# Finishing a float64 conversion on VectorE, and float32 operands used directly in two batches' attention

## The chip, the cores and the metric

The kernel runs on one core of a Trainium2 chip. The metric is the device time of one launch in microseconds, as the median of several runs. The core's engines have short names in the profile: PE is TensorE (PEld its weight loads), DVE is VectorE, ACT is ScalarE, POOL is GpSimd and SP is SyncE, which here only issues transfers. Each engine works through its own list of instructions in order, and waits for the others by semaphores.

## The reference

Attention goes through 32 packs per head, and two feed-forwards follow it. The weights (`w_in`, `w_out`, `w1` to `w3` and the second `w_out`) are float64 arrays; q, k, v and p are float32.

```python
p_packed = sm_attn(p, k, v)            # 8 batches, 8 heads, 576 tokens, 64 wide, 32 packs
out = sm_attn(q, p_packed, p_packed)
x = out.transpose(0, 2, 1, 3).reshape(4608, 512)
h = x @ w_in                           # 512 x 2048
g = h * (1.0 / (1.0 + np.exp(-1.702 * h)))
x = g @ w_out                          # 2048 x 512
h = np.maximum(np.maximum(x @ w1, x @ w2), x @ w3)   # 512 x 768 each
return (h @ w_out2).astype(np.float32)
```

## The kernel before

A float32 product is made of three passes over exact halves: an operand is split into a high half (a ScalarE cast to float32r) and a low half (what is left, by a subtraction), and `mm3` (lines 91 to 94) issues low times high, high times low, and high times high. `split` (112 to 114) does the subtraction on GpSimd, `evac` (116 to 118) does it on VectorE for a product that leaves PSUM.

The attention of four heads of a batch is a `Group`. Its steps are: load p and k (`load_pk`), put p into a block-diagonal tile `pbd` and split k (`split_pk`), load v, the scores of the packs `s1` with their softmax `sm1`, split v, transpose the weights into `et` (`t1`, `t1r`), the packed values `pv`, load and split q, transpose the packed values into `pt` (`pt`), the scores of the tokens `s2`, their softmax (`sm2`, `sm3`), and a transpose into `at` (`tr2`), which is split too. There are 16 groups; those of batches 0 and 1 (four) come first.

The weights arrive as the raw bits of float64, 1024 numbers per partition at a time. `convert` makes the two halves of such a block: four VectorE instructions over 1024 elements (lines 135, 138, 141, 143), two ScalarE instructions (136, 146), and two more over 1024 elements that finish the low half: an integer addition (147) on GpSimd and a subtraction (148) on GpSimd, or on VectorE in the first three blocks. Four blocks are needed for each quarter of the first feed-forward's hidden features (`wi0_n`, `wi1_n`, and two `wo`): 16 in all, and 12 blocks of the second feed-forward follow later (`tmp_w`).

The first feed-forward runs over 256 units, each of 288 tokens and 128 hidden features. `h_unit` makes the products `h` (6 matmuls, from `at` and from `pw`, the packed values times the first weights), a tanh on ScalarE (443) and a multiplication on VectorE (444). `g_unit` splits the result into two halves, with the cast on ScalarE (449) and the subtraction on VectorE (450). `out_unit` adds 12 matmuls to the accumulators `acc`. Batches 0 and 1 take turns in the first 128 units, so that conversions can keep up. The second feed-forward has 54 units of `h2_unit` and `out2_unit`.

All steps are written into a plan with a time each and issued in the order of these times; the tables `D_`, `W_`, `K_`, `L_` and others set them, and they are the same before and after. The tile framework then orders the instructions of each engine by its own estimate of their costs. Buffers come from pools: `w` (16 tiles, for raw weights, scratch and converted halves), `u` (18 tiles), and `ur` (6 tiles, for raw k, v and q).

Of the kernel before, what the change touches and what calls it, by code (L numbers as in the profile page):

```python
# [8 lines left out]
F32 = mybir.dt.float32  # L9
# [30 lines left out]
def tile_packed_attention_moe(  # L40
# [31 lines left out]

    # [128, 2, 2, 512]: the halves of two float32 operands, or scratch
    def w_tile(name, dt=F32R):
# [13 lines left out]

    # float32 products as three passes of exact 12-bit halves: lo*hi + hi*lo + hi*hi
    def mm3(o, a, b, start, stop):  # L90
# [4 lines left out]

# [1 line left out]
    ident = const.tile([P, P], F32, name="ident")  # L97
# [12 lines left out]

# [1 line left out]
    def split(raw, hi, lo):  # L112
# [6 lines left out]

    # A float64 is sign, 11 bits of exponent and 52 of fraction. Its high half is the sign, the  # L120
    # exponent moved to float32's bias (0 below its range) and 11 bits of fraction; with the next
    # bits, rounded to 12, added to its last place it is the float32, and the low half is the rest.
    def load_raw(name, srcs):
# [5 lines left out]
    def convert(name, raw, pool):  # L129
        h = raw.rearrange("p x a (b w) -> p (x a b) w", w=2)[:, :, 1]  # L130
        m = raw.bitcast(U16).rearrange("p x a (b w) -> p (x a b) w", w=4)[:, :, 1]
        tmp = w_tile(f"tmp_{name}", I32)
        t1, t2 = (tmp[:, x].rearrange("p a b -> p (a b)") for x in range(2))
        w = w_tile(name)
        nc.vector.tensor_scalar(out=t1, in0=h, scalar1=0x7FFFFE00, scalar2=None, op0=ALU.bitwise_and)
        nc.scalar.activation(t1, t1, AF.Relu, scale=8.0, bias=rebias)
        yield
        nc.vector.tensor_scalar(
            out=t2, in0=h, scalar1=0x1FF, scalar2=3, op0=ALU.bitwise_and, op1=ALU.logical_shift_left
        )  # L140
        nc.vector.scalar_tensor_tensor(out=t2, in0=m, scalar=2.0 ** -13, in1=t2, op0=ALU.mult, op1=ALU.add)
        yield
        nc.vector.scalar_tensor_tensor(
            out=t1, in0=h, scalar=-2 ** 31, in1=t1, op0=ALU.bitwise_and, op1=ALU.bitwise_or
        )
        nc.scalar.copy(w[:, :, 0], f(tmp[:, 0]))
        nc.gpsimd.tensor_tensor(out=t2, in0=t2, in1=t1, op=ALU.add)
        (nc.vector if pool & 1 else nc.gpsimd).tensor_tensor(
            out=w[:, :, 1], in0=f(tmp[:, 1]), in1=f(tmp[:, 0]), op=ALU.subtract
        )  # L150
        yield w

# [1 line left out]
    at = {}  # L154
# [3 lines left out]
    class Group:  # L158
# [8 lines left out]

        def split_pk(self):
            t = u_tile(f"pbd_{self.n}", F32R)
            nc.gpsimd.memset(f(t), 0.0)  # L170
# [14 lines left out]
        def load_t(self, src, name):  # L185
            raws = []
            for c in range(2):
                raws.append(ur_tile(f"raw_{name}_{self.n}_{c}"))
                nc.sync.dma_start(raws[-1], src[self.b, 2 * self.g + c])
            return raws  # L190
# [9 lines left out]
        def load_v(self):  # L200
            self.vraw = []
            for c in range(3):
                raw = ur_tile(f"raw_v_{self.n}_{c}")
                if c < 2:
                    nc.sync.dma_start(raw[:, :TB], v[self.b, self.g, :, c])
                else:
                    nc.sync.dma_start(raw[D:, :2 * P], vr[self.b, self.g])
                self.vraw.append(raw)

        def split_v(self):  # L210
            self.v = []
            for c in range(3):
# [11 lines left out]

        def split_q(self):
            self.q = self.split_t(self.qraw, "q")

        # scores of the packs, [4 heads x 32 packs, 288 keys]
        def s1(self, hf):
            o = pa_tile(f"s1_{self.n}_{hf}")  # L230
            hs = slice(hf * HALF, hf * HALF + HALF)
            for c in range(2):
                mm3(
                    o[:, :HALF], [t[:, c * P:c * P + P] for t in self.pbd],
# [24 lines left out]

        # weights of the packs with keys on partitions  # L260
        def t1(self):
            self.et = [ap_.tile([P, 5 * P], F32R, tag=f"et{x}", name=f"et{x}_{self.n}") for x in range(2)]
            o = pa_tile(f"t1_{self.n}")
            for c in range(4):
                nc.tensor.transpose(o[:, c * P:c * P + P], self.e1[:, c * P:c * P + P], ident)
            evac(o, self.et[0][:, :TB], self.et[1][:, :TB])

        def t1r(self):
            o = pa_tile(f"t1r_{self.n}")
            nc.tensor.transpose(o[:, :P], self.e1[:, S - P:S], ident)  # L270
            evac(o[D:, :P], self.et[0][D:, TB:], self.et[1][D:, TB:])

        # packed values, block-diagonal over the four heads
        def pv(self):
            o = pa_tile(f"pv_{self.n}")
            for c in range(5):
                r = slice(D if c == 4 else 0, P)
                vs = slice(c % 2 * 2 * P, c % 2 * 2 * P + 2 * P)
                mm3(
                    o[:, :2 * P], [t[r, c * P:c * P + P] for t in self.et],  # L280
# [7 lines left out]
        def pt(self):  # L288
# [6 lines left out]
            if self.b < 2:  # L295
                ptt[self.b, self.g] = self.ptt
                return
            # beside the packs of the other batch of the pair
            key = self.b // 2, self.g
# [8 lines left out]

        # scores of the tokens, [4 heads x 32 packs, 288 tokens], then tokens on partitions
        def s2(self, hf):  # L310
            o = pa_tile(f"s2_{self.n}_{hf}")
            hs = slice(hf * HALF, hf * HALF + HALF)
            for c in range(2):
                mm3(
                    o[:, :HALF], [t[:, c * P:c * P + P] for t in self.ptt],
# [26 lines left out]

        # weights of the tokens with packs on partitions
        def tr2(self):
# [5 lines left out]

        # (delay in us, step) of the whole group
        def steps(self):
# [4 lines left out]

# [1 line left out]
    wi = {}  # L359
# [20 lines left out]

    # the same for one batch
    def pw1_unit(b, g, n):
# [14 lines left out]

# [1 line left out]
    wo = {}  # L399
    gt, acc = {}, {}  # L400

    # units of the first feed-forward: (batch, half of its tokens, chunk of hidden features). Batches
    # 0 and 1 take turns by ranges of the chunks, so that the weights' conversions keep up.
    PAT = {
# [78 lines left out]

# [1 line left out]
    w3, wo2 = {}, {}  # L485
# [56 lines left out]

# [1 line left out]
    plan = []  # L544
# [36 lines left out]
    def main():  # L581
        HU = 2.2
        T0 = 39
        # startup
        attention(0.0, 0, 0, 1.07)
# [53 lines left out]

        # first feed-forward  # L640
        for pr in range(1, B // 2):
# [14 lines left out]

        # second feed-forward
        def w2_store(fc, x):
# [83 lines left out]
```

## Time and profile before

| | before |
|---|---|
| median of 3 runs | 1472.63 us (1471.9 to 1473.1) |
| span of the profiled execution | 1471.5 us |
| PE busy | 1391.3 us (95%), 8178 matmuls |
| PEld busy | 1257.4 us (85%) |
| DVE busy | 814.9 us (55%), 1355 instructions |
| ACT busy | 548.1 us (37%) |
| POOL busy | 421.2 us (29%), 351 instructions |

The span runs from the first to the last instruction of the profiled execution. Its own time is not recorded apart from that; the shown runs stand 0.4 to 1.6 us above the span. The busy shares are averages over a start, in which attention and conversions run, and a long remainder, in which hardly anything but matmuls goes on; they must be read stage by stage.

### The profile page before, as it was taken

How to read it: one execution, taken by the hardware profiler on the slowest of the kernel's cores; microseconds unless marked ns; L12 is line 12 of the kernel's file. 1: busy time of each engine (PE TensorE's matmuls, PEld its weight loads, DVE VectorE, ACT ScalarE, POOL GpSimd, SP SyncE). 2: the span in 40 equal slices, each digit the busy share in tenths (PEclk: the TensorE clock that was granted, in tenths of full speed). 3: DMA queues.
4: the chain of work that ended last, by engine and by line, in shares of the span. 5: the costliest groups of instructions: out<-in, count | busy, mean ns of one | idle time of the engine just before them, and what ended most of it. 6: DMA issues, size and time to landing. Idle time of an engine off the chain costs nothing.

```text
span 1471.5 us, 20929 instructions
## 1 busy us (share of the span) xinstructions
PE 1391.3 (95%) x8178; PEld 1257.4 (85%) x8178; DVE 814.9 (55%) x1355; ACT 548.1 (37%) x1134; POOL 421.2 (29%) x351
## 2 busy tenths in 40 slices
PE   3698788999999999999999999999999999999998
PEld 2587788999999999999999888888888888888887
DVE  6989998787675767666447997212122222222222
ACT  4454455555554555555444543112111111112011
POOL 7755675533431233520002466101011010101000
PEclk9799899999999999999999999999999999999999
DMA  7453323354323233332112232101010110100000
GB/s 251 166 187 138 143 90 90 121 176 121 119 80 97 93 96 98 92 102 88 60 55 94 86 137 92 59 4 57 0 58 15 43 29 29 43 0 30 1 29 29
DMA packets 53475, 121.42 MB, mean 83 GB/s; under 512 B 7296, under 2 KB 16512, under 8 KB 53376
## 3 DMA queue, kind: packets, MB, share of 16 engines
q1 hardware_dynamic: 44288, 86.52, 17.7%
q0 software_dynamic: 9088, 33.56, 6.9%
q8 instruction: 64, 1.05, 0.3%
q14 instruction: 35, 0.29, 0.1%
HBM read 92.80 MB, written 27.26 MB: 82 GB/s over the span
## 4 chain that ended last, share of the span: by engine, by line
PE 77%; DVE 16%; issue 3%; ACT 2%; POOL 2%; DMA 1%; SPq 0%; POOLq 0%; ACTq 0%; DVEq 0%
PE hb L94 10%; PE hb L93 10%; PE hb L92 10%; PE acc L92 7%; PE acc L93 7%; PE acc L94 7%; PE h L92 3%; PE accb L94 3%; PE accb L92 3%; PE accb L93 3%; PE h L94 3%; PE h L93 3%; DVE g L450 3%; DVE t L444 1%; DVE pw L118 1%
## 5 line engine op out<-in xcount | busy, mean ns | idle before, releaser
L92 PE MATMUL acc<-g,wo 128*128 128x288 f32 x1024 | 307.6, 301 | 3.8 <-ACT g L449 1.4
L93 PE MATMUL acc<-g,wo 128*128 128x288 f32 x1024 | 303.9, 297 | 6.6 <-DVE g L450 6.5
L94 PE MATMUL acc<-g,wo 128*128 128x288 f32 x1024 | 302.8, 296 | 0.0
L518 DVE TENSOR_TENSOR m<-hb,m 128x512 f32<-128x512 f32 x108 | 74.7, 691 | 393.0 <-PE hb L94 392.7
L94 PE MATMUL hb<-x,w 128*128 128x512 f32 x648 | 252.1, 389 | 0.0
L93 PE MATMUL hb<-x,w 128*128 128x512 f32 x648 | 252.1, 389 | 0.0
L92 PE MATMUL hb<-x,w 128*128 128x512 f32 x648 | 252.1, 389 | 0.0
L93 PEld LDWEIGHTS acc<-g,wo 128*128 128x128 f32 x1024 | 195.1, 191 | 11.9 <-DVE g L450 9.3
L450 DVE TENSOR_TENSOR g<-t,g 128x288 fp32r<-128x288 f32 x254 | 169.4, 668 | 61.9 <-ACT g L449 58.3
L92 PEld LDWEIGHTS acc<-g,wo 128*128 128x128 f32 x1024 | 194.8, 190 | 9.7 <-ACT g L449 2.5
L94 PEld LDWEIGHTS acc<-g,wo 128*128 128x128 f32 x1024 | 194.7, 190 | 0.3
L92 PE MATMUL h<-at,pw 128*128 128x288 f32 x512 | 155.6, 304 | 11.7 <-DVE t L444 11.0
L449 ACT CAST g<-t 128x288 fp32r<-128x288 f32 x256 | 110.6, 432 | 140.8 <-DVE t L444 139.8
L114 POOL TENSOR_TENSOR x<-x2raw,x 128x512 fp32r<-128x512 f32 x36 | 50.2, 1426 | 380.2 <-ACT x L113 380.2
L444 DVE SCALAR_TENSOR_TENSOR t<-t,h 128x288 f32<-128x288 f32 x256 | 114.9, 449 | 77.8 <-ACT t L443 76.0
L443 ACT ACTIVATE t<-h 128x288 f32<-128x288 f32 x256 | 104.7, 410 | 136.6 <-PE h L94 135.0
L93 PE MATMUL h<-at,pw 128*128 128x288 f32 x512 | 152.5, 298 | 1.4 <-POOL at L114 1.4
L94 PE MATMUL h<-at,pw 128*128 128x288 f32 x512 | 152.4, 298 | 0.0
L92 PEld LDWEIGHTS hb<-x,w 128*128 128x128 f32 x648 | 121.7, 188 | 25.2
L94 PEld LDWEIGHTS hb<-x,w 128*128 128x128 f32 x648 | 121.6, 188 | 25.3
L93 PEld LDWEIGHTS hb<-x,w 128*128 128x128 f32 x648 | 121.6, 188 | 25.2
L92 PEld LDWEIGHTS h<-at,pw 128*128 128x128 f32 x512 | 97.6, 191 | 14.8 <-DVE t L444 12.5
(133 smaller groups left out, 2324.2 us busy)
## 6 DMA issues: line engine op xcount, KB each, us to landing
wi<-wsc POOLq DMA_DIRECT2D x48, 512.0 KB, 3.6
raw_k<-in_k SPq DMA_DIRECT2D x32, 288.0 KB, 3.0
raw_q<-in_q SPq DMA_DIRECT2D x32, 288.0 KB, 2.8
x2d<-x SPq DMA_DIRECT2D x16, 576.0 KB, 3.4
x2raw<-x2d SPq DMA_DIRECT2D x36, 256.0 KB, 2.7
raw_w<-in_w SPq DMA_DIRECT2D x18, 512.0 KB, 4.3
out<-o SPq DMA_DIRECT2D x36, 256.0 KB, 2.1
raw_wi<-in_w_in SPq DMA_DIRECT2D x16, 512.0 KB, 6.8
```

Of the source, the lines that this page charges most:

```text
L92: nc.tensor.matmul(o, al, bh, start=start, stop=False)
L93: nc.tensor.matmul(o, ah, bl, start=False, stop=False)
L94: nc.tensor.matmul(o, ah, bh, start=False, stop=stop)
L114: nc.gpsimd.tensor_tensor(out=lo, in0=raw, in1=f(hi), op=ALU.subtract)
L118: nc.vector.tensor_tensor(out=lo, in0=o, in1=f(hi), op=ALU.subtract)
L443: nc.scalar.activation(t, o, AF.Tanh, scale=0.5 * 1.702)
L444: nc.vector.scalar_tensor_tensor(out=t, in0=t, scalar=1.0, in1=o, op0=ALU.add, op1=ALU.mult)
L449: nc.scalar.copy(g[:, 0], gt[n])
L450: (nc.gpsimd if n < 2 else nc.vector).tensor_tensor(out=g[:, 1], in0=gt[n], in1=f(g[:, 0]), op=ALU.subtract)
L518: nc.vector.tensor_tensor(out=t, in0=o, in1=t, op=ALU.max)
```

## The change

Two things change. First, `convert`: the nine low bits of the float64's high word and the next 16 bits of its fraction become one float32 number of 25 bits (line 139 now multiplies the 16 bits by 2^-16 and adds the nine bits). A VectorE instruction masks sign and exponent out of the high half and writes them over the raw bits (145), and another multiplies the 25 bits by this power of two and by 2^-20 to give the low half (146). The two instructions that stood on GpSimd (147 and 148 of before, in three blocks one of them on VectorE) are gone.

Second, in batches 0 and 1 the attention's products take float32 operands as they are, in one matmul where there were three. k, v and q of these four groups are no longer split. `pbd` and `et` hold one float32 copy, and the transposed packed values get a float32 copy (`ptf`, in the buffer of `pbd`) beside their halves, which `pw1_unit` still needs. The raw v and q of these groups move from the pool `ur` to the pool `u`.

```diff
@@ convert
-        nc.vector.tensor_scalar(
-            out=t2, in0=h, scalar1=0x1FF, scalar2=3, op0=ALU.bitwise_and, op1=ALU.logical_shift_left
-        )
-        nc.vector.scalar_tensor_tensor(out=t2, in0=m, scalar=2.0 ** -13, in1=t2, op0=ALU.mult, op1=ALU.add)
+        nc.vector.tensor_scalar(out=t2, in0=h, scalar1=0x1FF, scalar2=None, op0=ALU.bitwise_and)
+        nc.vector.scalar_tensor_tensor(out=f(t2), in0=m, scalar=2.0 ** -16, in1=t2, op0=ALU.mult, op1=ALU.add)
...
         nc.scalar.copy(w[:, :, 0], f(tmp[:, 0]))
-        nc.gpsimd.tensor_tensor(out=t2, in0=t2, in1=t1, op=ALU.add)
-        (nc.vector if pool & 1 else nc.gpsimd).tensor_tensor(
-            out=w[:, :, 1], in0=f(tmp[:, 1]), in1=f(tmp[:, 0]), op=ALU.subtract
+        nc.vector.tensor_scalar(out=h, in0=t1, scalar1=-2 ** 23, scalar2=None, op0=ALU.bitwise_and)
+        nc.vector.scalar_tensor_tensor(
+            out=w[:, :, 1], in0=f(tmp[:, 1]), scalar=2.0 ** -20,
+            in1=f(raw).rearrange("p x a (b w) -> p x (a b) w", w=2)[:, :, :, 1], op0=ALU.mult, op1=ALU.mult
         )
@@ split_pk
+            if self.b < 2:
+                t = u_tile(f"pbd_{self.n}")
+                nc.gpsimd.memset(t[:, :2 * P], 0.0)
+                for x in range(2):
...
+                    nc.vector.tensor_copy(to, self.praw[r])
+                self.pbd = t
+                return
@@ load_t, load_v
-                raws.append(ur_tile(f"raw_{name}_{self.n}_{c}"))
+                raws.append((u_tile if self.b < 2 and name == "q" else ur_tile)(f"raw_{name}_{self.n}_{c}"))
...
-                raw = ur_tile(f"raw_v_{self.n}_{c}")
+                raw = (u_tile if self.b < 2 else ur_tile)(f"raw_v_{self.n}_{c}")
@@ split_v, split_q
+            if self.b < 2:
+                return
@@ s1 (pv and s2 alike, with et and vraw, ptf and qraw)
+                if self.b < 2:
+                    nc.tensor.matmul(
+                        o[:, :HALF], self.pbd[:, c * P:c * P + P], self.kraw[c][:, hs], start=c == 0, stop=c == 1
+                    )
+                    continue
@@ t1 (t1r alike)
+            if self.b < 2:
+                nc.scalar.copy(self.et[:, :TB], o)
+                return
@@ pt
+                self.ptf = self.pbd[:, :2 * P]
+                nc.scalar.copy(self.ptf, o[:, :2 * P])
```

On GpSimd, the first rows after the constants are these before. `k`, `v` and `q` are the low halves of group (batch, group of heads), and `tmp_` is the scratch of a conversion:

```order
L170 MEMSET pbd_0_107 128x576
L114 TENSOR_TENSOR k_0_0_0_114<-raw_k_0_0_103,k_0_0_0_113 128x576
L114 TENSOR_TENSOR k_0_0_1_118<-raw_k_0_1_105,k_0_0_1_117 128x576
L170 MEMSET pbd_1_153 128x576
L114 TENSOR_TENSOR k_0_1_0_160<-raw_k_1_0_149,k_0_1_0_159 128x576
L114 TENSOR_TENSOR k_0_1_1_164<-raw_k_1_1_151,k_0_1_1_163 128x576
L147 TENSOR_TENSOR tmp_wi_0_179<-tmp_wi_0_179 128x1024
L114 TENSOR_TENSOR v_0_0_0_206<-raw_v_0_0_167,v_0_0_0_205 128x512
L114 TENSOR_TENSOR v_0_0_1_210<-raw_v_0_1_169,v_0_0_1_209 128x512
L607 DMA wsc<-wi_0_180 128x2x1024
```

The same place of the change, which is also all that GpSimd has up to the second group's `at`:

```order
L170 MEMSET pbd_0_107 128x256
L170 MEMSET pbd_1_135 128x256
L645 DMA wsc<-wi_0_152 128x2x1024
L170 MEMSET pbd_0_257 128x256
L645 DMA wsc<-wi_0_283 128x2x1024
L114 TENSOR_TENSOR at_0_0_314<-at_0_311,at_0_0_313 128x576
L114 TENSOR_TENSOR at_0_1_403<-at_1_400,at_0_1_402 128x576
```

The splits and the conversion's addition have left this engine; memsets, stores and the split of `at` stay.

On VectorE, the end of the first conversion and the start of the second stand so before, between the second group's `pbd` and the first group's `et`:

```order
L141 SCALAR_TENSOR_TENSOR tmp_wi_0_179<-raw_wi_0_121,tmp_wi_0_179 128x1024
L180 CAST pbd_1_153<-praw_1_147 64x2x32
L255 TENSOR_SCALAR st_0_0_131<-st_0_0_131 128x1
L181 TENSOR_TENSOR pbd_1_153<-praw_1_147,pbd_1_153 64x2x32
L258 RECIPROCAL st_0_0_131<-st_0_0_131 128x1
L180 CAST pbd_1_153<-praw_1_147 64x2x32
L143 SCALAR_TENSOR_TENSOR tmp_wi_0_179<-raw_wi_0_121,tmp_wi_0_179 128x1024
L181 TENSOR_TENSOR pbd_1_153<-praw_1_147,pbd_1_153 64x2x32
L118 TENSOR_TENSOR et_0_0_190<-t_0_0_191,et_0_0_189 128x512
L118 TENSOR_TENSOR et_0_0_190<-t1r_0_198,et_0_0_189 64x128
L135 TENSOR_SCALAR tmp_wo_243<-raw_wo_173 128x1024
L148 TENSOR_TENSOR wi_0_180<-tmp_wi_0_179 128x2x512
```

In the change the same place reads:

```order
L139 SCALAR_TENSOR_TENSOR tmp_wi_0_151<-raw_wi_0_111,tmp_wi_0_151 128x1024
L263 TENSOR_SCALAR st_0_0_117<-st_0_0_117 128x1
L141 SCALAR_TENSOR_TENSOR tmp_wi_0_151<-raw_wi_0_111,tmp_wi_0_151 128x1024
L174 COPY pbd_1_135<-praw_1_129 64x2x32
L272 TENSOR_SCALAR st_0_0_117<-st_0_0_117 128x1
L174 COPY pbd_1_135<-praw_1_129 64x2x32
L145 TENSOR_SCALAR raw_wi_0_111<-tmp_wi_0_151 128x1024
L275 RECIPROCAL st_0_0_117<-st_0_0_117 128x1
L146 SCALAR_TENSOR_TENSOR wi_0_152<-tmp_wi_0_151,raw_wi_0_111 128x2x512
L135 TENSOR_SCALAR tmp_wo_193<-raw_wo_145 128x1024
```

The two instructions at 145 and 146 are new and finish the block at once; the subtractions for `pbd` (181) and `et` (118) are gone.

## Rows read from the trace of the kernel before

**Rows 1.** By stretch: busy PE, PEld, DVE, ACT, POOL; clock, DMA share, GB/s.

```profile
0.00:79.30 79.30, 39.17 (x165) 32.56 (x166) 63.27 (x82) 35.14 (x64) 57.89 (x48) 0.85 0.56 194
79.30:232.40 153.10, 128.82 (x811) 120.80 (x811) 146.38 (x200) 74.77 (x145) 95.39 (x54) 0.91 0.38 138
232.40:300.00 67.60, 65.67 (x462) 61.69 (x460) 51.88 (x113) 39.53 (x92) 34.74 (x39) 1.00 0.39 120
...
780.00:912.00 132.00, 126.66 (x824) 117.17 (x823) 115.72 (x160) 61.44 (x115) 66.17 (x28) 1.00 0.29 102
```

**Rows 2.** What PE waited for, 80 to 260 us: total us, times, longest.

```profile
PE h L92 <- DVE t L444: 10.5, 5, 4.4
PE acc L93 <- DVE g L450: 5.0, 5, 2.4
```

**Rows 3.** What DVE waited for, 0 to 80 us.

```profile
DVE pbd L180 <- POOL pbd L170: 5.0, 2, 2.9
```

**Rows 4.** Timeline of DVE around 132 us: start us, us, instruction.

```profile
132.07 2.53 DVE L135 TENSOR_SCALAR tmp_wo<-raw_wo 128x1024 int32<-128x1024 int32 x1
134.53 2.60 DVE L450 TENSOR_TENSOR g<-t,g 128x288 fp32r<-128x288 f32 x1
```

**Rows 5.** Timeline of POOL in the same place.

```profile
131.50 2.56 POOL L147 TENSOR_TENSOR tmp_wo<-tmp_wo 128x1024 int32<-128x1024 int32 x1 [9.90 <-DVE tmp_wo L141]
134.13 2.68 POOL L148 TENSOR_TENSOR wo<-tmp_wo 128x1024 fp32r<-128x1024 f32 x1
```

**Rows 6.** Single lines of DVE: count, duration in ns (least/median/most).

```profile
L450 DVE TENSOR_TENSOR g<-t,g x254: 416/459/2647, 88.4 to 878.0; 128x288 fp32r<-128x288 f32 x127
...
L138 DVE TENSOR_SCALAR tmp_wi<-raw_wi x8: 644/682/1747, 11.4 to 184.3; 128x1024 int32<-128x1024 int32 x8
...
L141 DVE SCALAR_TENSOR_TENSOR tmp_wi<-raw_wi,tmp_wi x8: 1210/1220/2424, 12.1 to 185.2; 128x1024 int32<-128x1024 uint16 x8
```

**Rows 7.** Instructions on `tmp_wi` by stretch: DVE, ACT and POOL us (count).

```profile
0.00:79.30 79.30, 13.97 (x10) 4.40 (x4) 4.77 (x2) 0.85 0.56 194
79.30:232.40 153.10, 31.69 (x24) 13.22 (x12) 30.79 (x12) 0.91 0.38 138
```

**Rows 8.** The same for `tmp_wo`.

```profile
0.00:79.30 79.30, 15.06 (x9) 4.39 (x4) 7.54 (x3) 0.85 0.56 194
79.30:232.40 153.10, 34.28 (x24) 13.18 (x12) 30.04 (x12) 0.91 0.38 138
```

**Rows 9.** The same for `tmp_w`, the second feed-forward's blocks.

```profile
780.00:912.00 132.00, 59.54 (x48) 26.45 (x24) 60.05 (x24) 1.00 0.29 102
```

**Rows 10.** DVE's groups by form, 0 to 79.3 us: count, busy us, mean ns.

```profile
L180 DVE CAST pbd<-praw 64x64 fp32r<-64x64 f32 x8 | 7.9, 984 | 5.6 <-POOL pbd L170 5.0 <-DMA praw<-in_p 0.4
L181 DVE TENSOR_TENSOR pbd<-praw,pbd 64x64 fp32r<-64x64 f32 x8 | 4.6, 569 | 0.2
...
L339 DVE TENSOR_TENSOR a<-a,st 128x576 f32<-128x576 f32 x2 | 3.4, 1724 | 0.1
```

**Rows 11.** Instructions on `et`, 0 to 79.3 us: PE, PEld, DVE, ACT.

```profile
0.00:79.30 79.30, 10.18 (x45) 9.23 (x45) 2.93 (x6) 2.54 (x6) 0.85 0.56 194
```

**Rows 12.** DVE's groups by form, 79.3 to 232.4 us.

```profile
L450 DVE TENSOR_TENSOR g<-t,g 128x288 fp32r<-128x288 f32 x34 | 34.7, 1027 | 1.3 <-ACT g L449 1.2
...
L327 DVE TENSOR_TENSOR a<-a,st 128x576 f32<-128x576 f32 x3 | 4.8, 1593 | 0.0
...
L339 DVE TENSOR_TENSOR a<-a,st 128x576 f32<-128x576 f32 x2 | 1.5, 746 | 0.0
...
L180 DVE CAST pbd<-praw 64x64 fp32r<-64x64 f32 x4 | 0.8, 189 | 2.2 <-POOL pbd L170 2.1
```

**Rows 13.** Timeline of PE near the start: two passes of a score, and four transposes.

```profile
8.50 0.44 PE L94 MATMUL s<-k,pbd 128*128 128x288 f32 x1
8.74 0.44 PE L92 MATMUL s<-k,pbd 128*128 128x288 f32 x1
...
12.88 1.17 PE L265 MATMUL t<-ident,e 128*128 128x128 f32 x4 [3.22 <-ACT e L251]
```

More of the change, by code (lines that the diff above doesn't have):

```diff
@@ L168, in split_pk @@
         def split_pk(self):
+            if self.b < 2:
+                t = u_tile(f"pbd_{self.n}")
+                nc.gpsimd.memset(t[:, :2 * P], 0.0)
+                for x in range(2):
+                    r = slice(D * x, D * x + D)
+                    to = t[r, :384].rearrange("p (a b) -> p a b", b=192)[:, :, NP * x:NP * x + NP]
+                    nc.vector.tensor_copy(to, self.praw[r])
+                self.pbd = t
+                return
             t = u_tile(f"pbd_{self.n}", F32R)
@@ L261, in t1 @@
         def t1(self):
-            self.et = [ap_.tile([P, 5 * P], F32R, tag=f"et{x}", name=f"et{x}_{self.n}") for x in range(2)]
+            if self.b < 2:
+                self.et = ap_.tile([P, 5 * P], F32, tag="et0", name=f"et_{self.n}")
+            else:
+                self.et = [ap_.tile([P, 5 * P], F32R, tag=f"et{x}", name=f"et{x}_{self.n}") for x in range(2)]
             o = pa_tile(f"t1_{self.n}")
@@ L265, in t1 @@
                 nc.tensor.transpose(o[:, c * P:c * P + P], self.e1[:, c * P:c * P + P], ident)
+            if self.b < 2:
+                nc.scalar.copy(self.et[:, :TB], o)
+                return
             evac(o, self.et[0][:, :TB], self.et[1][:, :TB])
@@ L270, in t1r @@
             nc.tensor.transpose(o[:, :P], self.e1[:, S - P:S], ident)
+            if self.b < 2:
+                nc.scalar.copy(self.et[D:, TB:], o[D:, :P])
+                return
             evac(o[D:, :P], self.et[0][D:, TB:], self.et[1][D:, TB:])
@@ L278, in pv @@
                 vs = slice(c % 2 * 2 * P, c % 2 * 2 * P + 2 * P)
+                if self.b < 2:
+                    nc.tensor.matmul(
+                        o[:, :2 * P], self.et[r, c * P:c * P + P], self.vraw[c // 2][r, vs], start=c == 0, stop=c == 4
+                    )
+                    continue
                 mm3(
@@ L313, in s2 @@
             for c in range(2):
+                if self.b < 2:
+                    nc.tensor.matmul(
+                        o[:, :HALF], self.ptf[:, c * P:c * P + P], self.qraw[c][:, hs], start=c == 0, stop=c == 1
+                    )
+                    continue
                 mm3(
```

## The prediction

> **What bounds the kernel now.** I read the busy time by stretch first, then the waits of the engine that idles, then single instructions. The stretches are cut where the work changes: at 79.3 us, where the first feed-forward product reaches DVE, and at 232.4 us, just after the last of the first 16 conversions. Call them A (0 to 79.3) and B (79.3 to 232.4). In A, PE is busy 39.2 of 79.3 us and DVE 63.3; in B, PE 128.8 of 153.1 us and DVE 146.4; from 232.4 on, PE is busy 65.7 of 67.6 us [rows 1]. So up to 232 us DVE has the most to do, and later PE does. The waits agree: in B, PE's longest are on DVE's product for h (10.5 us) and on its split of g (5.0 us) [rows 2]. What PE gains before 232 us is kept, for afterwards it is full whatever came before.
>
> Why DVE is so busy is seen in single instructions. The subtraction at line 450 takes 0.459 us in the middle and 2.647 at worst, with the same shape [rows 6]. At 132.07 us a mask (line 135) takes 2.53 us and the subtraction behind it 2.60 us [rows 4]; meanwhile POOL runs its two conversion steps, from 131.50 to 134.06 and from 134.13 to 136.81 [rows 5]. The mask ends at 134.60 and the subtraction at 137.13, each 0.3 to 0.5 us after a POOL instruction ended: about what such an instruction takes alone, or less. DVE stood there, counted as busy, until POOL was done. So part of DVE's 146.4 us is not work but POOL's time, and the change takes most of POOL's work away.
>
> **The change, part by part.** One profiled execution gives the durations. Its span is 1471.5 us, and the median of the runs is 1472.6, so I add 1.1 us at the end for what lies around the span.
>
> *Conversions.* A block had four DVE instructions and two on POOL. It now has six on DVE. Free of POOL, a mask over 1024 numbers takes 0.68 us (line 138's middle value) and a two-input instruction 1.22 us (line 141's) [rows 6]. The new mask (line 145) is shown nowhere: it writes every second word where lines 135 and 138 read every second word. Its ends are 0.68 us, as those, and 1.22 us, as the slowest instruction over 1024 numbers when undisturbed. I take 0.68, because it has line 135's layout turned round. The new multiplication (146) has a two-input instruction's row, 1.22. A block is then 3 x 0.68 + 3 x 1.22 = 5.7 us, at most 6.2.
> In A there are four blocks, which took DVE 14.0 + 15.1 = 29.0 us [rows 7, 8], the three subtractions at 148 within it; now 22.8: 6.2 saved. In B there are twelve, which took 31.7 + 34.3 = 66.0 us [rows 7, 8]; now 68.5: 2.5 lost, or 8.9 with the slow mask. Two more DVE instructions per block thus cost nearly nothing, if POOL leaves the others alone: of the 66.0 us, 66.0 - 12 x (2 x 0.68 + 2 x 1.22) = 20.4 was stretch.
>
> *Attention of batches 0 and 1.* In A, the copies and subtractions for `pbd` took 7.9 + 4.6 us [rows 10]. Eight copies at 0.19 us, as in B [rows 12], make 1.5: 11.0 saved. The `et` subtractions, 2.9 us for three groups [rows 11], go, and about 1.0 in B for the fourth. Line 339 falls from 3.4 us [rows 10] to two at 0.75 [rows 12]: 1.9 saved.
> On POOL, all splits of k, v and q of four groups go, so that memsets no longer stand behind them; DVE waited 5.0 us for such a memset in A [rows 3]. I count half of it, 2.5 us, since DVE then comes sooner to something else that is not there yet. ACT loses casts and gains one copy per group; with 35.1 of 79.3 us busy [rows 1] it hides that; uncovered, a copy would be worth less than one of the casts that go.
>
> *Other DVE work in B.* 34 subtractions at line 450 fall from 34.7 us [rows 12] to 34 x 0.459 = 15.6: 19.1 saved. Line 327 falls from 4.8 us to three at 0.75: 2.6 saved [rows 12]. The stretch in B is 19.1 + 20.4 + 2.6 = 42.1 us. It does not all go: of POOL's 95.4 us [rows 1] the conversions are 60.8 [rows 7, 8], and of the other 34.6, those for group (1, 1) go, while the splits of batches 2 and 3 stay. I keep a quarter of the stretch, 10.5 us (36%, 15.3 us, if all 34.6 stayed; nothing if they meet no DVE instruction).
>
> *Products.* 156 matmuls (39 for each of four groups) become 52. No row shows a float32 product of this size. A pass follows its neighbour by 0.24 us at the start [rows 13]; the nearest rows with float32 operands are the transposes, four in 1.17 us, at most 0.29 us for 128 columns [rows 13]. The ends are one pass, 0.24 us, and four passes, 0.96. Scaled by columns the transposes give 0.66 for 288, between them, and 0.66 for one is a little less than 0.72 for three passes. So I take no gain and no loss on PE, which has 40 idle us in A and 24 in B [rows 1]. The longer case is a rival below.
> The Trainium skill (FP8 and Floating Point Precision, TensorE Precision Notes) says that a true float32 product takes four passes through the array. No row shows it; by it, 52 products are 208 passes in place of 156, an estimate of 12 us more for PE at the early pace, and about 1444 us if half of that lies on the path.
>
> *Late conversions.* Twelve blocks fall between 780 and 912 us. They took DVE 59.5 us [rows 9] and will take 68.5, 9.0 more. DVE idles 132.0 - 115.7 = 16.3 us there [rows 1], and POOL's 60.1 us [rows 9] no longer stretch its neighbours. I count nothing; without that relief it would still fit, and with no idle time it would cost the 9.0.
>
> *Queues and buffers.* SP's loads of v and q no longer wait for POOL to release their `ur` tiles, and a raw weight tile is held until line 146 instead of 143, but POOL's steps, which held its scratch, are gone. I count both at nothing: earlier data only helps where DVE is not the last.
>
> **Sum.** A: 6.2 + 11.0 + 2.9 + 1.9 + 2.5 = 24.5 us. B: -2.5 + 1.0 + 19.1 + 2.6 - 10.5 = 9.7 us. Together 34.2: the span becomes 1437.3 us, and the time 1438.4 us, of which I say 1438. With the bounds (slow mask: 6.4 in B and 2.2 in A less; stretch kept 0 to 15.3; the memset wait 0 to 5.0) this case reaches from 1425 to 1454.
>
> **Rivals.**
> *PE or the loads set the start.* If a float32 product is four passes, a group's score, values and score take 8 x 0.96 + 5 x 0.85 = 12 us at the early pace instead of 39 x 0.23 = 9; three groups lie in A, one behind the other, and each step waits for a softmax. With 3 us each and as much again from DVE waiting for them, A gives about 9 less and B the same: 1447. Against it stands PE's idle half of A. Chance 20%.
> *PE takes over in B.* If the kept stretch is small and DVE's waits in A shrink too, PE becomes the bound in B. PE had 128.8 us there, in which a matmul is often slow or waits at a granted clock of 0.91; at the later pace (462 matmuls in 65.7 us [rows 1], 0.142 each) 811 take 115, which would save 38 in B; with waits between the engines I put it at 26, together 50: 1422. Chance 16%.
> *The stretch is not POOL's.* Then each of DVE's six instructions costs what one did on average. In A that is 29.0 / 19 = 1.53 us, 36.7 for 24, 7.7 more, which the 4.6 and 2.9 us of the subtractions that go make up for. In B, 66.0 / 48 = 1.37 us, so 24 new ones add 33, less 1.0. Late, 59.5 / 48 = 1.24 us, so 24 add 30 against 16.3 idle: 13. Together 45 slower, 1518 us. Between my 34 saved at a quarter kept and this, the sign changes when a little over half of the stretch stays. Rows 4 and 5 speak against it. Chance 6%.
> *The change does little*: the new steps run, but data or buffers hold the same places, within 0.2%: 2%.
>
> **How the numbers follow.** The main case has 56%. The predicted time is 1438 us. From 1414 to 1456 us lie the main case, the first rival and most of the second; what is left out is the deeper part of the second and the last two, and error in the sizes. 0.2% (3 us) is about what can be told from no change here. Faster 0.92, same 0.02, slower 0.06.
>
> **What would show it.** In the profile after, POOL has far less to do in the first 230 us, line 450's subtractions there take close to 0.46 us, the masks 0.68, line 145 too, and line 146 about 1.2. The first t comes about 25 us earlier, near 55 us, and the end of the sixteenth conversion some 34 us earlier, near 198. The prediction is wrong if DVE's instructions stay long with POOL quiet, if line 145 or 146 takes twice its row, or if PE waits for its own products in A.

## The result, and the profile after

| | before | after |
|---|---|---|
| median of 4 runs, us | 1472.27 (1470.53 to 1473.10) | 1436.82 (1434.98 to 1437.92) |
| profiled span, us | 1471.5 | 1433.0 |

The ratio is 0.976, 95% interval 0.9746 to 0.9773: 35.5 us faster, and 1 us below the 1438 forecast. The profiled execution took 1434.98 us, the fastest of its four, so its span is 38.5 shorter where the medians differ by 35.5: some 3 us between the two traces is the spread of the runs and not the change.

The first t reaches DVE at 59.1 us (79.3 before), and the last of the first 16 conversions is over at 203.9 (232.4 before). So A is now 0 to 59.1 and B 59.1 to 203.9. Busy time by stretch of the kernel after, in the columns of [rows 1], with the late conversions last:

```profile
0.00:59.10 59.10, 39.26 (x125) 25.53 (x125) 38.72 (x71) 22.79 (x44) 7.07 (x20) 1.00 0.76 273
59.10:203.90 144.80, 127.92 (x832) 118.39 (x832) 135.49 (x235) 79.39 (x157) 30.57 (x28) 0.96 0.41 145
...
741.00:872.00 131.00, 126.66 (x845) 120.23 (x844) 114.36 (x188) 62.88 (x118) 6.13 (x4) 0.99 0.30 103
```

In A, DVE's busy time fell by 63.3 - 38.7 = 24.6 us, but its idle time rose from 16.0 to 20.4, which leaves 20.2. In B it fell from 146.4 to 135.5. POOL fell from 57.9 to 7.1 in A and from 95.4 to 30.6 in B. What DVE waits for in A, beside [rows 3]:

```profile
DVE st L259 <- PE s L246: 5.5, 3, 3.8
DVE pbd L174 <- POOL pbd L170: 4.8, 2, 2.6
DVE pn L315 <- PE pv L306: 3.0, 3, 1.9
DVE a L358 <- PE s L348: 2.8, 3, 1.9
```

The memset wait is as long as before (4.8 and 5.0 us). The other three, 11.3 us, wait for float32 products. In the kernel before, DVE waited 5.8 us for products in A, nearly all of it here:

```profile
DVE st L242 <- PE s L94: 5.5, 2, 4.7
```

So the waits for products grew by 5.5 us. Single lines of DVE in the kernel after, in the columns of [rows 6]; line 488 is the old 450:

```profile
L488 DVE TENSOR_TENSOR g<-t,g x254: 416/458/1830, 64.3 to 841.4; 128x288 fp32r<-128x288 f32 x127
...
L145 DVE TENSOR_SCALAR raw_wi<-tmp_wi x8: 653/697/1547, 13.6 to 155.9; 128x1024 int32<-128x1024 int32 x8
...
L146 DVE SCALAR_TENSOR_TENSOR w<-tmp_w,raw_w x12: 1218/1226/2308, 754.0 to 870.6; 128x1024 fp32r<-128x1024 f32 x12
```

The mask that was shown nowhere (line 145) takes 0.70 us and the multiplication (146) 1.23 at the middle. Conversions by stretch in the columns of [rows 7 to 9] (DVE and ACT now, no POOL): `tmp_wi` in A and B, `tmp_wo` in A and B, then `tmp_w` late:

```profile
0.00:59.10 59.10, 11.38 (x12) 4.39 (x4) 1.00 0.76 273
59.10:203.90 144.80, 36.42 (x36) 13.23 (x12) 0.96 0.41 145
...
0.00:59.10 59.10, 11.22 (x12) 4.40 (x4) 1.00 0.76 273
59.10:203.90 144.80, 38.02 (x36) 13.23 (x12) 0.96 0.41 145
...
741.00:872.00 131.00, 69.81 (x72) 26.43 (x24) 0.99 0.30 103
```

DVE's groups by form, from A and then from B, beside [rows 10] and [rows 12]:

```profile
L174 DVE COPY pbd<-praw 64x64 f32<-64x64 f32 x8 | 1.5, 192 | 4.9 <-POOL pbd L170 4.8
...
L488 DVE TENSOR_TENSOR g<-t,g 128x288 fp32r<-128x288 f32 x36 | 16.8, 471 | 0.1
```

36 subtractions take 16.8 us where 34 took 34.7. A float32 product, which no row showed, in PE's timeline, beside [rows 13]: at the start, and at 60 us between passes over the same 288 columns.

```profile
4.16 4.54 PE L246 MATMUL s<-raw_k,pbd 128*128 128x288 f32 x8 [4.16 <-DMA raw_k<-in_k]
...
59.99 0.29 PE L94 MATMUL h<-at,pw 128*128 128x288 f32 x1
60.13 0.29 PE L92 MATMUL h<-at,pw 128*128 128x288 f32 x1
60.26 2.10 PE L246 MATMUL s<-raw_k,pbd 128*128 128x288 f32 x8
```

Four products show as eight instructions. How far apart they start is read from the length of a run and of one instruction, first in the last four at the start, then in the eight at 60 us:

```profile
6.58 2.13 PE L246 MATMUL s<-raw_k,pbd 128*128 128x288 f32 x4
L246 PE MATMUL s<-raw_k,pbd x4: 687/687/687, 6.6 to 8.0; 128*128 128x288 f32 x4
...
L246 PE MATMUL s<-raw_k,pbd x8: 403/406/406, 60.3 to 62.0; 128*128 128x288 f32 x8
```

At the start that is (2.13 - 0.69) / 3 = 0.48 us for an instruction, 0.96 for a product, where passes follow by 0.24 [rows 13]. At 60 us it is (2.10 - 0.41) / 7 = 0.24 and 0.48, where a pass follows the next by 0.13. So a product is four passes at the start, and 3.6 of the passes beside it at 60 us. The granted clock is 1.00 from 4 to 9 us and from 59 to 62 us, so it does not show why the early ones take twice as long. The Trainium skill (FP8 and Floating Point Precision, TensorE Precision Notes) states four passes for a true float32 product; the trace agrees at the start.

What PE waits for from 59 to 230 us, beside [rows 2]:

```profile
PE acc L92 <- DVE x L508: 5.9, 3, 3.6
PE acc L93 <- DVE g L488: 5.2, 2, 2.9
PE h L92 <- DVE t L482: 3.3, 4, 1.4
```

PE still waits for DVE most, 14.4 us in these three rows; what it waits for ScalarE and GpSimd is 1.5 us. DVE is still the bound up to the sixteenth conversion.

To see where time is won or lost I take the start of ACT's tanh, one for each of the 256 units of the first feed-forward, counted from 0. Start of the n-th in the profiled execution, read from ACT's timeline (us):

```
n            0     16     36     40     64    100    130    140    230    240    253
before    76.9  137.9  225.9  243.9  329.9  446.1  525.5  565.1  806.2  833.9  870.7
after     58.7  111.7  191.4  207.4  296.0  412.2  491.6  529.7  770.7  795.1  833.5
e1        70.0  129.6  212.6  227.8  316.9  433.0  512.4  550.5  791.5  815.9  856.0
e2        57.1  118.8  206.2  224.3  310.0  426.1  505.6  545.2  786.3  814.0  850.8
e3        71.9  130.6  238.4  254.5  345.8  461.8  541.2  580.8  826.2  860.6  903.4
e4        55.1  104.5  170.9  186.0  272.1  388.3  467.7  505.8  746.8  770.9  802.0
e5        54.0  108.6  191.4  206.4  295.7  411.9  491.3  529.4  770.4  794.8  834.8
e6        59.7  112.2  195.7  210.2  299.1  415.3  494.7  534.3  775.3  799.7  839.6
e7        59.0  110.7  185.7  203.3  290.8  406.5  490.0  529.5  770.5  794.6  834.8
e8        57.0  109.5  183.8  198.4  287.2  403.5  482.9  521.0  762.0  786.4  824.7
e9        57.0  108.5  179.8  194.3  284.4  400.3  482.2  520.3  761.3  785.4  825.5
e10       57.9  110.5  184.7  199.3  286.9  405.7  485.9  522.9  766.9  791.5  829.9
```

After against before: 18.2 us ahead at the first, 26.2 at the 16th, 36.5 at the 40th, 33.9 from the 64th to the 130th, 37.2 at the 253rd. Nearly all is won by the 40th.

### The profile page after: what moved, and what is told of

The parts are those of the page before. It is cut to its first block, busy times and chain, and to the rows that moved or that the text cites. A ratio compares the mean times of both kernels' runs of the same rounds, so it can differ in the third digit from the quotient of the medians.

```text
span 1433.0 us, 20661 instructions
## 1 busy us (share of the span) xinstructions
PE 1383.3 (97%) x8126; PEld 1244.7 (87%) x8126; DVE 771.8 (54%) x1392; ACT 535.4 (37%) x1110; POOL 241.0 (17%) x270
## 3 DMA queue, kind: packets, MB, share of 16 engines
q1 hardware_dynamic: 44288, 86.52, 18.2%
## 4 chain that ended last, share of the span: by engine, by line
PE 86%; DVE 10%; issue 1%; ACT 1%; DMA 0%; SPq 0%; POOL 0%; ACTq 0%; DVEq 0%; POOLq 0%
PE hb L94 10%; PE hb L93 10%; PE hb L92 10%; PE acc L92 8%; PE acc L93 8%; PE acc L94 8%; PE h L92 4%; PE h L94 4%; PE h L93 4%; PE accb L93 3%; PE accb L94 3%; PE accb L92 3%; DVE g L488 1%; PE pw L92 1%; PE pw L93 1%
## 5 line engine op out<-in xcount | busy, mean ns | idle before, releaser
L488 DVE TENSOR_TENSOR g<-t,g 128x288 fp32r<-128x288 f32 x254 | 140.4, 554 | 53.8 <-ACT g L487 50.2
L559 ACT CAST gb<-m 128x512 fp32r<-128x512 f32 x54 | 33.5, 620 | 203.9 <-DVE m L556 203.9
```

What stands on the lines that cost most here:

```text
L488: (nc.gpsimd if n < 2 else nc.vector).tensor_tensor(out=g[:, 1], in0=gt[n], in1=f(g[:, 0]), op=ALU.subtract)
L559: nc.scalar.copy(g[0], t)
```

## The experiments

**e1 and e2: each half alone.** e1 is the kernel before with the new conversion; e2 is the kernel after with the old one (its diff is this one turned round).

```diff
-        nc.vector.tensor_scalar(
-            out=t2, in0=h, scalar1=0x1FF, scalar2=3, op0=ALU.bitwise_and, op1=ALU.logical_shift_left
-        )
-        nc.vector.scalar_tensor_tensor(out=t2, in0=m, scalar=2.0 ** -13, in1=t2, op0=ALU.mult, op1=ALU.add)
+        nc.vector.tensor_scalar(out=t2, in0=h, scalar1=0x1FF, scalar2=None, op0=ALU.bitwise_and)
+        nc.vector.scalar_tensor_tensor(out=f(t2), in0=m, scalar=2.0 ** -16, in1=t2, op0=ALU.mult, op1=ALU.add)
...
-        nc.gpsimd.tensor_tensor(out=t2, in0=t2, in1=t1, op=ALU.add)
-        (nc.vector if pool & 1 else nc.gpsimd).tensor_tensor(
-            out=w[:, :, 1], in0=f(tmp[:, 1]), in1=f(tmp[:, 0]), op=ALU.subtract
+        nc.vector.tensor_scalar(out=h, in0=t1, scalar1=-2 ** 23, scalar2=None, op0=ALU.bitwise_and)
+        nc.vector.scalar_tensor_tensor(
+            out=w[:, :, 1], in0=f(tmp[:, 1]), scalar=2.0 ** -20,
+            in1=f(raw).rearrange("p x a (b w) -> p x (a b) w", w=2)[:, :, :, 1], op0=ALU.mult, op1=ALU.mult
```

> The kernel before with the new conversion alone: six VectorE instructions per block, none on GpSimd; attention as before, all splits of k, v and q on GpSimd. Theory (GpSimd's instructions stretch VectorE's): the start keeps its splits, so that the first t comes only some 6 us earlier than before (near 73 us), and the stretch up to the sixteenth conversion shrinks because 61 of GpSimd's 95 us there go: together 15 to 20 us faster than before, near 1454. Rival (the gain is attention's lighter work, and two more VectorE instructions per block cost what they take): no faster than before, up to 20 us slower.

> The changed kernel with the old conversion: GpSimd adds and subtracts for every block again; attention of batches 0 and 1 with float32 operands. Theory: the start gains most of its 20 us (no splits on GpSimd; pbd and et lighter), less what two GpSimd instructions per block stretch there: 12 to 18 us, first t near 64 us. From there to the sixteenth conversion little is gained. Near 1455. Rival (the conversion is all): within 5 us of 1472.

e1: 1458.2 us (1455.63 to 1460.51), ratio 0.9906 [0.989, 0.9923], 13.5 faster. e2: 1454.81 us (1452.72 to 1457.12), 0.9884 [0.9869, 0.99], 16.9 faster. Together 30.4 of the 35: nearly additive. Where each wins is in the table: e2 is 19.8 us ahead at the first tanh and stays near there (19.6 at the 40th); e1 is 6.9 ahead at the first and 16.1 at the 40th. With both, the first is 18.2 ahead: in A the conversions add nothing to what the attention gives, and in B they give what the attention does not. Busy time from 79.3 to 203.9 us in e1:

```profile
79.30:203.90 124.60, 109.07 (x695) 101.40 (x693) 114.18 (x189) 67.88 (x130) 27.82 (x22) 0.93 0.44 160
```

and in e2:

```profile
79.30:203.90 124.60, 100.94 (x631) 94.05 (x631) 117.17 (x156) 57.73 (x112) 73.43 (x42) 0.92 0.34 119
```

With POOL at 73 us DVE carries out 156 instructions in 117.2 us; with POOL at 28, 189 in 114.2. The conversion with two more DVE instructions gets more of them through. The subtraction of `g_unit` in the same stretch, in e1 and in e2:

```profile
L449 DVE TENSOR_TENSOR g<-t,g 128x288 fp32r<-128x288 f32 x31 | 14.6, 472 | 0.8 <-ACT g L448 0.7
L489 DVE TENSOR_TENSOR g<-t,g 128x288 fp32r<-128x288 f32 x30 | 24.4, 816 | 1.5 <-ACT g L488 1.5
```

The same instruction takes 0.47 us in e1 and 0.82 in e2.

**e3: POOL's steps put back, with nothing waiting for them.** Behind line 146 POOL adds two scratch tiles of the block that are no longer needed, twice.

```diff
+        nc.gpsimd.tensor_tensor(out=t2, in0=t2, in1=t1, op=ALU.add)
+        nc.gpsimd.tensor_tensor(out=t2, in0=t2, in1=t1, op=ALU.add)
```

> The changed kernel with two GpSimd additions over 1024 numbers put behind every block's last VectorE instruction; they rewrite scratch that nobody reads any more, so nothing waits for their result except the scratch buffer's next use. Theory: 24 such additions up to the sixteenth conversion lengthen VectorE's instructions beside them by about 1 us each, 15 to 24 us in all, and the late 12 blocks give back 3 us more: 1455 to 1463. Rival (the long instructions of before had another cause): 1437, within 3 us.

1508.13 us (1501.42 to 1509.33), ratio 1.0237 [1.0212, 1.0261]: 71 us slower than the kernel after, so the direction was right, and the size that was expected about a third of it. DVE's groups by form in e3, 60 to 240 us, with the same subtraction as above, now line 490:

```profile
L490 DVE TENSOR_TENSOR g<-t,g 128x288 fp32r<-128x288 f32 x34 | 27.4, 811 | 0.1
...
L141 DVE SCALAR_TENSOR_TENSOR tmp_wi<-raw_wi,tmp_wi 128x1024 int32<-128x1024 int32 x6 | 11.6, 1941 | 0.0
L135 DVE TENSOR_SCALAR tmp_wi<-raw_wi 128x1024 int32<-128x1024 int32 x6 | 10.3, 1712 | 0.0
```

and POOL's:

```profile
L150 POOL TENSOR_TENSOR tmp_wi<-tmp_wi 128x1024 int32<-128x1024 int32 x6 | 14.8, 2464 | 43.0 <-DVE wi L146 43.0
```

The subtraction is at 0.81 us, up from 0.47, and on the `wi` blocks the mask of line 135 is at 1.71 and line 141 at 1.94, up from about 0.7 and 1.22. 56 additions cost 71 us, 1.27 each, about half of one's own 2.4 to 2.6. By the table, 47 of the 71 are there at the 40th tanh, behind 32 additions. The additions also hold the block's scratch tiles longer. Up to the sixteenth conversion that is not what costs, as busy time from the first t to that conversion in e3 shows:

```profile
72.00:255.00 183.00, 145.54 (x852) 130.56 (x851) 177.28 (x242) 81.36 (x161) 90.06 (x52) 0.88 0.32 115
```

DVE idles 5.7 us of the 183, none of it for a scratch tile, and is busy 41.8 us longer than in B of the kernel after (135.5), with 242 instructions instead of 235. How much of the later 24 us is a wait for tiles, this run does not tell apart. That POOL's work makes DVE's instructions longer is seen in the rows themselves.

**e4: the mask and the multiplication left out.** The low halves are copied by ACT from the same scratch.

```diff
-        nc.vector.tensor_scalar(out=h, in0=t1, scalar1=-2 ** 23, scalar2=None, op0=ALU.bitwise_and)
-        nc.vector.scalar_tensor_tensor(
-            out=w[:, :, 1], in0=f(tmp[:, 1]), scalar=2.0 ** -20,
-            in1=f(raw).rearrange("p x a (b w) -> p x (a b) w", w=2)[:, :, :, 1], op0=ALU.mult, op1=ALU.mult
-        )
+        nc.scalar.copy(w[:, :, 1], f(tmp[:, 1]))
```

> The changed kernel without the two new VectorE instructions of a block; the low half is filled with a ScalarE copy of the scratch instead of the product, so the values are others. Theory (VectorE still sets the pace up to the sixteenth conversion, PE is close behind): 24 us less VectorE work in B and 8 in A, of which PE's own need lets about half through: 8 to 16 us faster, 1421 to 1429. Rival (PE has taken over): 0 to 4 us faster.

1408.24 us (1403.79 to 1408.57), ratio 0.9568 [0.9552, 0.9584]: 28.6 below the kernel after, more than either theory said. The two instructions take 0.70 + 1.23 = 1.93 us, 31 for 16 blocks. The table shows 3.6 us won at the first tanh, 21.4 at the 40th, 24 from the 64th to the 240th, and 31.5 at the 253rd. So up to the 40th some 0.7 of each microsecond taken from DVE comes off the time (for the whole edit, which also gives ScalarE a copy for each block and releases the raw weights a step earlier), and the late blocks, whose 12 x 1.93 = 23 us go, give 7. Busy time from 100 to 200 us in e4:

```profile
100.00:200.00 100.00, 96.44 (x679) 93.19 (x678) 91.62 (x171) 69.37 (x129) 29.28 (x30) 0.98 0.39 132
```

and in the kernel after:

```profile
100.00:200.00 100.00, 88.51 (x592) 83.05 (x591) 95.42 (x163) 55.94 (x108) 18.84 (x18) 0.97 0.36 128
```

In e4 PE becomes the fuller engine, at 96.4 of 100 us. In the kernel after, that takeover has not come: PE has 11.5 us free and DVE 4.6.

**e5: half of the float32 products left out.** One of each pair in the scores, and three of five in the values, remain. The edit for the scores of the packs; the others are alike:

```diff
-                    nc.tensor.matmul(
-                        o[:, :HALF], self.pbd[:, c * P:c * P + P], self.kraw[c][:, hs], start=c == 0, stop=c == 1
-                    )
+                    if c == 0:
+                        nc.tensor.matmul(o[:, :HALF], self.pbd[:, :P], self.kraw[c][:, hs], start=True, stop=True)
```

> The changed kernel with about half of the float32 products of batches 0 and 1 left out (one of two chunks of each score, three of five of the packed values), so other values; nothing else moves. Theory (a float32 product is four passes and the start waits for them): of VectorE's 11.3 us of waits for scores and packed values before the first t about half goes, the first t comes 4 to 6 us earlier, and the time falls to 1431 to 1434. Rival (the start's chain is made of VectorE's and ScalarE's steps, products lie beside them): within 2 us of 1437.

1436.19 us (1435.32 to 1439.1), ratio 0.9762 [0.9747, 0.9777]: no different from the kernel after. DVE's waits in the first 60 us of e5:

```profile
DVE pbd L174 <- POOL pbd L170: 4.8, 2, 2.6
DVE st L258 <- PE s L247: 3.4, 4, 2.4
DVE a L357 <- PE s L349: 2.9, 3, 2.2
```

The wait for values is all but gone (0.2 us), that for scores fell from 5.5 to 3.4, and the first tanh came 4.7 us earlier. At the 36th tanh the lead was nothing (191.4 in both). Busy time in e5's own B:

```profile
54.40:203.90 149.50, 129.44 (x822) 120.69 (x822) 138.10 (x236) 79.78 (x158) 30.78 (x28) 0.92 0.40 141
```

DVE idles 11.4 us of it where it idled 9.3, and is busy 2.6 us longer for about the same instructions (236, 235): 4.7 together, just the lead. So the products' length did set the start, and the lead was given back in B. Why it was, stays open.

**e6: the memset on DVE.** It has DVE fill `pbd` itself, so that it need not wait for POOL.

```diff
-                nc.gpsimd.memset(t[:, :2 * P], 0.0)
+                nc.vector.memset(t[:, :2 * P], 0.0)
```

> The changed kernel with the memset of pbd in batches 0 and 1 on VectorE in place of GpSimd, where it stands behind the split of at. Theory: VectorE's 4.8 us of waits for that memset go, for four memsets of some 0.3 us: 2 to 4 us faster, 1433 to 1435. Rival (VectorE then waits for the next thing, the first h): within 1.5 us of 1437.

1440.96 us (1440.47 to 1442.73), ratio 0.9793 [0.9779, 0.9807]: 4 slower than after, where 2 to 4 faster was expected. DVE's waits in the first 60 us of e6:

```profile
DVE st L259 <- PE s L246: 9.3, 5, 4.5
DVE a L358 <- PE s L348: 4.8, 6, 1.5
...
DVE pn L315 <- PE pv L306: 0.3, 1, 0.3
```

The memset wait (4.8) went, and the waits for products grew from 5.5 + 3.0 + 2.8 to 9.3 + 4.8 + 0.3: 3.1 more. The memset itself is new work for DVE. Busy time in the first 60 us of e6:

```profile
0.00:60.00 60.00, 37.74 (x125) 25.38 (x126) 41.15 (x78) 22.76 (x43) 6.05 (x16) 0.83 0.75 270
```

The granted clock is 0.83 where the kernel after shows 1.00 in its A, so PE was at its lower level, 1.2 GHz, for part of it. But the products took as long in both (the first group's values 4.93 us in each), so the clock does not account for the wait. What changed is DVE's order. The first conversion starts so in the kernel after, and so in e6:

```profile
9.11 0.69 DVE L135 TENSOR_SCALAR tmp_wi<-raw_wi 128x1024 int32<-128x1024 int32 x1 [1.83 <-DMA raw_wi<-in_w_in]
16.13 0.68 DVE L135 TENSOR_SCALAR tmp_wi<-raw_wi 128x1024 int32<-128x1024 int32 x1
```

In e6 the raw weights have landed at 9.1 us too, but the conversion stands behind the second group's scores, for which DVE waits 3.0 us and 1.1 us just before it. So this run does not show what the memset's wait alone is worth.

**e7: less on DVE elsewhere.** The low halves of `pw` (line 429) and the first stores of x2 (line 511) leave DVE for PE and ACT everywhere.

```diff
-        if n < 1 and b == 0:
+        if True:
...
-            elif dc % 2 == 0:
+            elif True:
```

> The changed kernel with some VectorE work up to the sixteenth conversion given to engines that idle: the low halves of pw of batches 0 and 1 by a matmul with the negative identity and a ScalarE copy (14 more places like the first two), and all first stores of x2 on ScalarE. VectorE loses 10 subtractions of 0.69 us and 8 multiplications of 0.45 us there. Theory (VectorE sets the pace, as the run without mask and product showed with 28 us for 32 instructions): 6 to 9 us faster, 1428 to 1431. Rival (ScalarE's added steps make its answers late): no faster.

1434.99 us (1433.87 to 1436.05), ratio 0.975 [0.9737, 0.9764], 1.8 below after: within what can be told here. The table shows 5.7 us ahead at the 36th and 100th tanh, 1.6 at the 130th, 0.2 at the 140th. What PE waits for from 400 to 545 us in e7, beside a stop of 2.5 us that the kernel after has too:

```profile
PE h L92 <- DVE t L482: 1.9, 1, 1.9
```

and busy time in two pieces of that stretch, in e7:

```profile
430.00:460.00 30.00, 28.14 (x195) 27.49 (x194) 22.50 (x40) 15.13 (x35) 6.93 (x8) 0.94 0.29 93
510.00:530.00 20.00, 17.47 (x114) 16.71 (x114) 15.43 (x30) 8.39 (x18) 3.83 (x6) 0.91 0.10 31
```

In the kernel after, the first of these has PE busy 30.00 of 30.00 us with 221 matmuls. One wait of 1.9 us, and a granted clock of 0.94 behind it, went with 26 matmuls fewer, some 3.4 us at 0.13. The granted clock lies between its two levels in the mean, so for part of the stretch it stood at 1.2 GHz. The second piece holds the stop of 2.5 us. The kernel after has it in the same place, at the full granted clock:

```profile
510.00:530.00 20.00, 17.47 (x126) 16.86 (x125) 16.48 (x33) 9.29 (x20) 3.82 (x6) 1.00 0.11 31
```

There e7 is 12 matmuls short, some 1.6 us. By the table the lead shrank by 4.1 us from the 100th to the 130th tanh and by 1.4 to the 140th, so the two places are nearly all of the loss. Why the wait falls there stays open.

**e8 and e10: float32 operands in more batches.** e8 uses them in batches 0 to 3, e10 in all eight; the copy of `pt` is made for all of them. One of twelve such lines:

```diff
-            if self.b < 2:
+            if self.b < 4:
```

> The changed kernel with float32 operands also in batches 2 and 3. GpSimd loses their splits, of which about 21 us lay before the sixteenth conversion, and VectorE the low halves of pbd and et. PE's products for four groups go from three passes to four, about 13 passes of 0.13 us, 1.7 us a group. Theory (what is left of the stretch there is GpSimd's splits, 6 us in the conversions): 4 to 7 us less up to there, 3 to 7 us more PE work in all: 1433 to 1438. Rival (products on a full PE decide): 1440 to 1444.

> The run with float32 operands to batch 3, with float32 operands in all eight batches. Theory (operands used directly pay where VectorE is the last and cost where PE is): batches 4 to 7 run while PE is full; eight groups of 13 passes of 0.13 us more make 14 us, so 1438 to 1444 in place of 1427. Rival (the lighter GpSimd and VectorE pay there too): within 4 us of 1427.

e8: 1427.27 us (1425.79 to 1428.51, 5 runs), ratio 0.9698 [0.9684, 0.9712], 9.5 below the kernel after and the fastest of those that leave nothing out. Busy time from 100 to 200 us in e8:

```profile
100.00:200.00 100.00, 93.47 (x611) 87.12 (x610) 94.88 (x169) 53.35 (x103) 5.75 (x11) 0.97 0.35 127
```

POOL has 5.8 us instead of 18.8, DVE gets 169 instructions through instead of 163 in the same time, and PE 611 matmuls instead of 592. By the table it is 1.7 ahead at the first tanh, 7.6 at the 36th and 8.7 from the 100th to the 240th.

e10: 1431.61 us (1430.1 to 1435.13), 0.973 [0.9717, 0.9744], 4.3 slower than e8. It loses from the 64th tanh (0.3 ahead) to the 230th (4.9 behind). Busy time from 500 to 740 us in e10:

```profile
500.00:740.00 240.00, 239.70 (x1691) 230.40 (x1691) 135.04 (x283) 107.89 (x252) 18.27 (x38) 1.00 0.25 78
```

and in e8:

```profile
500.00:740.00 240.00, 237.45 (x1753) 233.50 (x1752) 150.68 (x300) 119.23 (x273) 46.93 (x59) 1.00 0.26 80
```

PE is full in both, DVE has 105 us free in e10 and 89 in e8: here the longer products are on the path, and more free time on DVE is worth little. A product takes 0.48 us from start to start and three passes 0.40; 39 / 3 = 13 products per group and 8 groups make 0.08 x 104 = 8.3 us, where 14 were expected; it cost 4.9. PE's 2.25 us fewer idle in this stretch make up for some. They are the stop of 2.5 us, which e8 has here and e10 has not:

```profile
PE pw L92 <- issue: 2.5, 1, 2.5
```

The remaining 1.2 us are open.

**e9: e8 and e7 together.**

> The run with float32 operands to batch 3, with the VectorE work of e7 given to PE and ScalarE as well. Theory (VectorE sets the pace up to the sixteenth conversion; e7 was 5 to 6 us ahead at its units 44 to 100): 3 to 6 us faster than e8, 1421 to 1424. Rival (what e7 lost near its unit 116 comes with the same change, by a wait and a lower granted clock): 1425 to 1428.

1428.45 us (1426.8 to 1430.56, 5 runs), ratio 0.9709 [0.9696, 0.9723]: no faster than e8. It is 3.2 ahead of e8 at the 100th tanh and 0.7 at the 130th. What PE waits for from 400 to 545 us in e9, beside the stop of 2.5 us that e8 has too, and busy time around this wait:

```profile
PE h L92 <- DVE t L483: 1.9, 1, 1.9
430.00:460.00 30.00, 28.15 (x203) 27.36 (x203) 23.42 (x41) 16.01 (x36) 6.92 (x8) 1.00 0.36 112
```

e8 has 220 matmuls there, 17 more, some 2.2 us. So the wait of e7 came again and took most of the lead, this time without a lower granted clock.

## Why the prediction was right

**The mechanism held.** DVE was the engine with the most to do up to the last of the first 16 conversions, part of its busy time was POOL's, and what was gained there was kept (e7 and e9 show that a full PE does not keep every lead). Line 488 at 0.47 us in B, e3's rows, and e1's 189 instructions in less time than e2's 156 show the stretch. e4 shows that DVE's work sets the pace there. Of the forecast 34.2 us, the tanh shows 33.9 from the 64th to the 130th.

**A: 24.5 forecast, 20.2 measured.** The pieces of DVE's work came as priced: conversions 29.0 to 22.6 us (6.4, forecast 6.2), `pbd` 12.5 to 1.5 (11.0), `et` gone. Busy time fell by 24.6 where the terms without the memset wait make 22.0. Two steps failed. *"I count half of it, 2.5 us"* for the memset: nothing was saved (5.0 and 4.8). The first of the two waits ends at 2.6 us, ahead of the transfer of k that releases the first product at 4.16, so it had nothing to give; what the second is worth alone, no run shows. *"I take no gain and no loss on PE"*: a float32 product took 0.48 us where three passes take 0.40, and 0.96 at the start where three take 0.72, and DVE's waits for products rose from 5.8 to 11.3 us. That is the mechanism of the first rival. e1 and e2 say it too: in A the conversions' saving adds nothing beside the attention's. But e5 shows that A was not worth its full price to the end: 4.7 us there gave nothing. Where A ends is a choice: by the first tanh A gives 18.2 us and B 15.7.

**B: 9.7 forecast, 33.9 - 20.2 = 13.7 measured.** The stretch was priced too high. Conversions took DVE 36.4 + 38.0 = 74.4 us; undisturbed they were to take 68.5, so 5.9 are stretch; line 488 has 36 x (0.471 - 0.458) = 0.5. That is 6.4 of the 42.1, 15% and not a quarter, 4.1 us less than the 10.5 kept. By its own terms B gives: conversions -8.4 (66.0 to 74.4), `et` 1.0 as counted, line 488 17.9 (34.7 to 16.8, and two more of them), line 327 2.5 (now three at 0.77 us), together 13.0. The new mask was 0.70, near the 0.68 taken and far from 1.22; e4 shows that the upper end would have cost most of its price, since 21.4 of 31 us of DVE's time came off there. A and B missed by 4.3 and 4.0 in opposite senses, so that the sum came within 1.2 us of the measured time is luck. The 1.1 us added for what lies around the span was 2.0 in the profiled execution.

*"Near 198"* for the end of the sixteenth conversion was 203.9: 28.5 us earlier, not 34. The other 5 us are units of the feed-forward: 36 subtractions at line 488 lie ahead of that end, where 34 lay before, and two units take about 6 us (116.2 us from the 64th tanh to the 100th, 3.2 each).

**Late: nothing counted.** The blocks took DVE 69.8 us for 59.5, 10.3 more, of which 9.0 were forecast. The lead went from 35.5 at the 230th tanh to 37.2 at the 253rd; e1's was 14.7 at both. The cover named, DVE's idle time, held. It was thinner than the 16.3 us idle suggest: e4, with those blocks shorter, won 7 us there.

**The rivals.** *PE or the loads set the start* came in part: its mechanism is there, at less than its price. That price does not add up in its own terms either: three groups at 3 us and as much again are 18 us, and its time takes 9. *PE takes over in B* fell: PE waits 14.4 us for DVE there, and it is e4 that comes to it, at 1408. *The stretch is not POOL's* fell with e1 and e3. *The change does little* fell with the result.

## What to carry to other kernels

Where an engine's instructions are long now and then with the same shape, look for a POOL instruction that ends just ahead of their end: work moved from POOL to DVE can be faster though DVE has more of it, and e8 found more of the same gain in the next two batches. A product that costs PE a fifth to a third more is free only where PE waits for another engine; the same edit gave 9.5 us in batches 2 and 3 and cost 4.3 in batches 4 to 7. A wait in a start-up stage should be counted as saved only when the next thing waited for is already there, and a lead there can be lost in the next stage, as e5's 4.7 us were.

## What the runs showed of the hardware

POOL's additions of 2.4 to 2.6 us, which nothing needed, made DVE's 0.47 us subtraction 0.81 on average and the kernel 1.27 us longer for each (e3). The Trainium skill (SBUF — State Buffer, Who interferes with whom) has VectorE, in its two-port modes, contend with GpSimd for one shared pair of ports, which the one that issues first keeps for its whole instruction while the other stands. [rows 4, 5] agree: DVE's 0.68 us mask took 2.53 and ended 0.5 us behind POOL's 2.56 us addition.

A float32 product of 128 by 288 shows as two instructions and takes 0.48 us from start to start among passes that follow one another by 0.13; at the kernel's start it takes 0.96 among passes of 0.24. The granted clock is 1.00 in both places.

A single wait of 1.9 us on a full PE went with a granted clock of 0.94 over 30 us, and with 26 matmuls fewer than the 221 without it (e7). The same wait in e9 went with a granted clock of 1.00 and 17 fewer than e8's 220. A stop of 2.5 us that both kernels have went with 0.91 over 20 us in e7 and with 1.00 in the kernel after, 114 matmuls and 126.
